# Windowed attention: x transposed by DMA on its way in, queries reordered by their evacuation

## The chip, the cores and the metric

The kernel runs on one core of a Trainium2 chip. The metric is the device time of one execution in microseconds. TensorE (PE) multiplies matrices into PSUM, VectorE (DVE), ScalarE (ACT) and GpSimd (POOL) work element by element, and SyncE (SP) issues the DMAs.

## The reference

The input x is an image of 224 x 224 positions with 96 channels in bf16. The first 48 channels of q, k and v attend within 28 horizontal windows of 8 rows each; the other 48 attend within 28 vertical windows of 8 columns each. A window has 1792 tokens.

```python
qkv = jnp.einsum('bhwc,cd->bhwd', x, wqkv)
q, k, v = qkv[..., :C], qkv[..., C:2*C], qkv[..., 2*C:]
scale = C2 ** (-0.5)                                   # C2 = C // 2 = 48, sw = 8
qh = q[..., :C2].reshape(B * nh, sw * W, C2)           # kh, vh alike: horizontal windows
ah = softmax(einsum('bqc,bkc->bqk', qh, kh) * scale)
oh = einsum('bqk,bkc->bqc', ah, vh).reshape(B, H, W, C2)
qv = q[..., C2:].reshape(B, H, nw, sw, C2).transpose(0, 2, 1, 3, 4).reshape(B * nw, H * sw, C2)
av = softmax(einsum('bqc,bkc->bqk', qv, kv) * scale)   # kv, vv alike: vertical windows
ov = einsum('bqk,bkc->bqc', av, vv)                    # put back to B, H, W, C2
o = concat(oh, ov)                                     # written there as two pads and a sum
return jnp.einsum('bhwc,cd->bhwd', o, wo)
```

## The kernel before, in words

Two windows are worked on together, one in the upper and one in the lower half of the partitions. This makes 28 pairs P: 14 horizontal ones, then 14 vertical ones. `b = P % 2` chooses between two sets of buffers.

**Preparation of a pair (`prep`).** x of the pair is loaded into `x_sb` with its tokens on the partitions (`load`, L409 to L426): two DMAs a window for a horizontal pair, 14 for a vertical one. TensorE transposes it in four fills (`pe_fn`, L534 to L540), and VectorE copies each from PSUM to `xT_sb`, where channels are on the partitions (L526 for horizontal pairs, L532 for vertical ones). The horizontal copy also reorders the tokens, from row by row to blocks of 8 x 8 positions. Because a transpose works on 64 channels at a time, with the 96 channels read as 0 to 63 and 32 to 95, `xT_sb` has 128 channel rows, and the projection weights `w_sb` have zeros and gaps to match. From `xT_sb` come keys in four fills and queries in four fills (L551; chunks of 512, 512, 512 and 256 tokens), and values in four fills (L597). VectorE evacuates them: keys with a running sum (L565), queries by a plain copy (L561), values (L602). POOL subtracts the keys' mean (L576) and scales values for the second way of taking exponentials (L610). This is 16 fills in all.

**Attention.** A score unit is one 128-key tile against 512 queries (or two tiles against 256), for both windows. TensorE computes it into one of three ring slots of PSUM, two banks each (L762). Of each pair's 49 units, 42 go to ACT, which takes the exponential (L780), and 7 to VectorE, which builds an approximate exponential out of one scaling (L804) and four cheap additions to 16-bit integers that are read as bf16 (L814). TensorE then multiplies the results by the values (L745).

**Finishing.** VectorE evacuates the output of a chunk (L709). TensorE projects it with `wo` (L637 horizontal, L666 vertical), and VectorE divides by the sums (L625, L644, L673). Horizontal results stay in `Ph_sb`; for vertical pairs POOL adds them (L677), and SP stores the rows (L686).

**What sets the order.** Every instruction is an `Op` with estimated costs. The `Planner` places the ops one after the other on each engine, by readiness and priority, and so writes out a fixed order for every engine; at run time an engine works through its list and waits for semaphores. Preparation of pair P + 1 is spread over the attention of pair P: each fill has a soft dependence on the start of one of ACT's exponentials (`pace`, L845). Fills take either an output bank or half a ring slot (`FillPool`). Loads and stores share SP's queue. `load(P + 2)` is issued when pair P's transposes have read `x_sb` (`t_pe`, L423).

Of the kernel before, what the change touches and what calls it, by code (L numbers as in the profile page):

```python
# [245 lines left out]
def bass_standalone__window_attn_cswin__vision_kernel(  # L246
# [19 lines left out]
    TH, FTH = 112, 8  # L266
    RPF = FTH * TH // W
# [6 lines left out]
    with es:  # L274
# [5 lines left out]
        ident = sb("ident", [128, 128], BF16)  # L280
        ident_f = sb("ident_f", [128, 128], FP32)
# [3 lines left out]
        x_sb = [sb(f"x_sb{i}", [128, 2, 16, C], BF16) for i in range(2)]  # L285
# [29 lines left out]
        s_x = [[[sem(f"s_x{b}{w}{hf}") for hf in range(2)] for w in range(2)] for b in range(2)]  # L315
# [70 lines left out]
        for v in range(2):  # L386
            for w in range(2):
                o_wov0 = first("dve", 0.15, lambda e, v=v, w=w: e.memset(wo_sb[v][w][:], 0.0))
        o_one = first("dve", 0.1, lambda e: e.memset(one_sb[:], 1.0))
        o_iota = first("pool", 0.3, lambda e: e.iota(ident_f[:], [[1, 128]], base=0, channel_multiplier=-1,  # L390
                                                     allow_small_or_imprecise_dtypes=True))
        o_ident = first("dve", 0.2, lambda e: e.tensor_single_scalar(ident[:], ident_f[:], 0.0, ALU.is_equal), [o_iota])
# [8 lines left out]
        x_flat = x[0].rearrange("h w c -> (h w) c")  # L401
        x_vtiles = x[0].rearrange("(kt hh) (j dw) c -> j kt hh dw c", hh=16, dw=8)
# [4 lines left out]
        t_pe = {P: [] for P in range(NP)}  # L407

        def load(P, stream):  # L409
            b = P % 2  # L410
            for w in range(2):
                src = x_flat[(2 * P + w) * NTOK:(2 * P + w + 1) * NTOK, :].rearrange("(k p) c -> p k c", p=TH) if is_h[P] else None
                for hf in range(2):
                    sm = s_x[b][w][hf]
                    own = x_tot.get((b, w, hf), 0)
                    if is_h[P]:
                        todo = [(x_sb[b][0:TH, w, hf * FTH:(hf + 1) * FTH, :], src[:, hf * FTH:(hf + 1) * FTH, :])]
                    else:
                        todo = [(x_sb[b][:, w, kt, :], x_vtiles[2 * (P - NPH) + w, kt])
                                for kt in range(8 * hf, min(NKT, 8 * hf + 8))]  # L420
                    for i, (dst, s_) in enumerate(todo):
                        op = Op("sp", 0.06, 2.2, lambda e, dst=dst, s_=s_: e.dma_start(dst, s_),
                                t_pe[P - 2] if P >= 2 and i == 0 else [], dma=(sm, own if i == 0 else 0))  # L423
                        stream.append(op)
                        x_op[(P, w, hf)] = op
                        x_tot[(b, w, hf)] = x_tot.get((b, w, hf), 0) + 16  # L426

        load(0, q_first["sp"])
        op_w0 = Op("sp", 0.7, 2.8, lambda e: e.dma_start(w_sb[0:64, :, 0:C2], wqkv.rearrange("c (s d) -> c s d", s=6)[0:64]), [o_w0], dma=(s_w0, 0))
        q_first["sp"].insert(1, op_w0)  # L430
        op_w0 = Op("sp", 0.7, 2.8, lambda e: e.dma_start(w_sb[96:128, :, 0:C2], wqkv.rearrange("c (s d) -> c s d", s=6)[64:96]), [o_w0], dma=(s_w0, 0))
        q_first["sp"].insert(2, op_w0)
# [71 lines left out]
        def prep(P, pace=None, startup=False):  # L504
# [7 lines left out]
            xt_w = {}  # L512
            qk_war = last_qk[prev2] if prev2 >= 0 else []
            pv_war = last_pv[prev2] if prev2 >= 0 else []
            xt_war = xt_read.get(prev2, [])
            xt_read[P] = []
            for w in range(2):
                for hf in range(2):
                    if is_h[P]:
                        tp, nt = TH, FTH  # L520
                        ks = [hf * FTH + j for j in range(FTH)]

                        def ev_fn(e, bk, op, w=w, hf=hf):
                            src = bk.bitcast(BF16)[:, 0:FTH * TH].rearrange("c (r bc dw) -> c r bc dw", r=RPF, dw=8)
                            dst = xT_sb[b][:, w, :].rearrange("c (bc r dw) -> c r bc dw", r=SW, dw=8)[:, hf * RPF:(hf + 1) * RPF, :, :]
                            return e.tensor_copy(dst, src)  # L526
                    else:
                        ks = list(range(8 * hf, min(NKT, 8 * hf + 8)))
                        tp, nt = 128, len(ks)

                        def ev_fn(e, bk, op, w=w, ks=ks):
                            return e.tensor_copy(xT_sb[b][:, w, ks[0] * 128:(ks[-1] + 1) * 128], bk.bitcast(BF16)[:, 0:len(ks) * 128])  # L532

                    def pe_fn(e, bk, w=w, ks=ks, tp=tp):  # L534
                        bkb = bk.bitcast(BF16)
                        for j, k in enumerate(ks):
                            for h in range(2):
                                ins = e.transpose(bkb[64 * h:64 * h + 64, j * tp:(j + 1) * tp], x_sb[b][0:tp, w, k, 32 * h:32 * h + 64],  # L538
                                                  ident[0:tp, 0:tp])
                        return ins  # L540
                    p, ops = fill(0.055 * nt, pe_fn, [x_op[(P, w, hf)], o_ident],
                                  [("dve", 0.07 + nt * tp / 1920, ev_fn, xt_war, True, dve_ev, [], None)], soft() + xt_war)
                    t_pe[P].append(p)
                    xt_w.setdefault(w, []).append(ops[0])
            xt_all = xt_w[0] + xt_w[1]
            prevk = []
            for kind in "kq":
                for c, (q0, qs) in enumerate(CH):
                    def pe_fn(e, bk, kind=kind, q0=q0, qs=qs):
                        for w in range(2):  # L550
                            ins = e.matmul(bk[64 * w:64 * w + 64, 0:qs], lhsT=w_sb[:, wblk(P, kind), :],  # L551
                                           rhs=xT_sb[b][:, w, q0:q0 + qs], start=True, stop=True)
                        return ins
                    if kind == "q":
                        if startup:
                            def ev_fn(e, bk, op, q0=q0, qs=qs):
                                return e.activation(QT_sb[b][:, q0:q0 + qs], bk[:, 0:qs], ACTF.Copy)
                            evs = [("act", 0.55, ev_fn, qk_war, True, q_first["act"], [], None)]
                        else:
                            def ev_fn(e, bk, op, q0=q0, qs=qs):  # L560
                                return e.tensor_copy(QT_sb[b][:, q0:q0 + qs], bk[:, 0:qs])  # L561
                            evs = [("dve", 0.07 + qs / 960, ev_fn, qk_war, True, dve_ev, [], None)]
                    else:
                        def ev_fn(e, bk, op, c=c, q0=q0, qs=qs):
                            return e.tensor_scalar(KT_sb[b][:, q0:q0 + qs], bk[:, 0:qs], 1.0, None,  # L565
                                                   ALU.mult, ALU.add, accum_out=ksum[b][:, c:c + 1])
                        evs = [("dve", 0.08 + qs / 960, ev_fn, qk_war, True, dve_ev, [], None)]
                        if c == NCH - 1:
                            def ev2(e, bk, op):
                                return e.tensor_scalar(kjunk[:, :], ksum[b][:, :], -1.0 / NTOK, None,  # L570
                                                       ALU.mult, ALU.add, accum_out=negmean[b][:, :])

                            def ev3(e, bk, op):
                                if startup:
                                    return e.tensor_scalar(KT_sb[b][:, :], KT_sb[b][:, :], negmean[b][:, 0:1], None, ALU.add)
                                return e.tensor_scalar(KT_sb[b][:, :], KT_sb[b][:, :], negmean[b][:, 0:1], 1.0, ALU.add, ALU.mult)  # L576
                            evs.append(("dve", 0.15, ev2, list(prevk), False, dve_ev, [], None))
                            evs.append(("dve", 0.6, ev3, [], False, dve_ev, [], None) if startup else
                                       ("pool", 1.8, ev3, [], False, pool_k, [], None))
                    p, ops = fill(0.43 * qs / 1024, pe_fn, xt_all + [op_w0], evs, soft() + qk_war)  # L580
                    xt_read[P].append(p)
                    if kind == "q":
                        q_ready[(P, c)] = ops[0]
                    else:
# [4 lines left out]
            for w in range(2):  # L589
                for k0 in range(0, NKT, VS):  # L590
                    n = min(VS, NKT - k0)

                    def pe_fn(e, bk, w=w, k0=k0, n=n):
                        for j in range(n):
                            for h in range(2):
                                t0 = (k0 + j) * 128 + 64 * h
                                ins = e.matmul(bk[64 * h:64 * h + 64, j * C2:(j + 1) * C2], lhsT=xT_sb[b][:, w, t0:t0 + 64],  # L597
                                               rhs=w_sb[:, wblk(P, "v"), 0:C2], start=True, stop=True)
# [4 lines left out]
                    p, ops = fill(0.045 * n, pe_fn, xt_w[w] + [op_w0, o_v1],  # L603
# [10 lines left out]
        xt_read = {}  # L614

# [215 lines left out]
        for P in range(NP):  # L831
# [11 lines left out]
            if P + 1 < NP:  # L843
                base = a_start[P]
                prep(P + 1, pace=lambda n, base=base: [act_of[base + int(n * NA * PACE / 16)]])  # L845
# [74 lines left out]
```

## Time and profile before

| what | value |
|---|---|
| median of 3 runs | 1147.38 us (1147.14 to 1147.86) |
| the profiled execution, its own time | 1150.81 us |
| its span in the profile | 1149.0 us |
| granted TensorE clock, mean | 0.991 |
| ACT busy | 1094.7 us |
| DVE busy | 977.8 us |
| PE busy | 1109.8 us |
| POOL busy | 198.3 us |
| DMA queue of SP, share of 16 engines | 13.8% |

Busy time is the union of an engine's instructions. Matmuls are pipelined and their ends are modelled, so a busy PE is not a PE at its peak. A group line gives the source line, the engine, what is written from what, the shape, and the count; after the bar come the busy time of the group, the mean duration of one instruction in ns, and the idle time of the engine just before such instructions with what ended it. PEld is TensorE's loading of stationary operands, which overlaps the matmuls. SPq is SP's issuing of DMAs.

### The profile page before, as it was taken

What the parts mean: (1) busy time and instruction counts of PE and PEld (TensorE: products, weight loads), DVE (VectorE), ACT (ScalarE), POOL (GpSimd) and SP (SyncE); (2) the same over time, 40 slices, a digit from 0 to 9 for tenths busy, and PEclk for the clock granted to TensorE, in tenths of its full rate; (3) what the DMA queues carried; (4) which work ended last, traced back from release to release, by engine and by line L of the source; (5) the groups of instructions that cost most, each with busy time, mean ns of one, the idle gap of its engine ahead of it and who ended that gap; (6) DMA issues with size and microseconds to landing.
All of it is one profiled execution on the core that took longest, in us unless ns stands there. A gap on an engine that the chain in (4) does not pass through costs nothing.

```text
span 1149.0 us, 30551 instructions
## 1 busy us (share of the span) xinstructions
PE 1109.8 (97%) x12888; PEld 459.3 (40%) x12888; DVE 977.8 (85%) x2138; ACT 1094.7 (95%) x1182; POOL 198.3 (17%) x256
## 2 busy tenths in 40 slices
PE   8999999999999999999999999999999999999996
PEld 3434433443443344344434433433443443344342
DVE  6898888798888978888888888898889988988974
ACT  5999999999999999999999999999999999999997
POOL 0101010010101001010112222222222313222121
PEclk7999999999999999999999999999999999999998
DMA  4011011101100110110111221121122212210011
GB/s 87 15 25 26 4 23 25 26 2 25 26 18 10 26 26 2 25 22 12 19 30 29 38 35 32 36 38 35 32 37 37 36 32 38 36 31 19 19 20 24
DMA packets 164977, 31.00 MB, mean 27 GB/s; under 512 B 164840, under 2 KB 164840, under 8 KB 164840
## 3 DMA queue, kind: packets, MB, share of 16 engines
q1 hardware_dynamic: 164840, 29.05, 13.8%
q8 instruction: 101, 1.65, 0.6%
q14 instruction: 36, 0.29, 0.1%
HBM read 19.36 MB, written 9.63 MB: 25 GB/s over the span
## 4 chain that ended last, share of the span: by engine, by line
PE 53%; DVE 25%; ACT 19%; issue 2%; DMA 0%; SPq 0%; ACTq 0%; POOL 0%; POOLq 0%
PE ps L745 24%; PE ps L762 19%; ACT PT L780 19%; DVE L_sb L814 10%; DVE Y_sb L804 7%; PE ps L538 4%; PE ps L551 3%; DVE OT_sb L709 2%; DVE KT_sb L565 2%; DVE tmp L673 2%; PE ps L597 2%; PE ps L637 1%; DVE QT_sb L561 1%; DVE V_sb L602 1%; PE ps L666 1%
## 5 line engine op out<-in xcount | busy, mean ns | idle before, releaser
L780 ACT ACTIVATE PT<-ps 128x1024 bf16<-128x1024 f32 x1176 | 1091.2, 1085 | 36.1 <-PE ps L762 26.1
L762 PE MATMUL ps<-QT_sb,KT_sb 48*128 48x512 bf16 (+1 forms) x3136 | 458.2, 357 | 8.5 <-DVE V_sb L602 1.7
L745 PE MATMUL ps<-PT,V_sb 128*64 128x512 bf16 (+1 forms) x2688 | 388.3, 360 | 0.7 <-ACT PT L780 0.7
L814 DVE TENSOR_SCALAR L_sb<-Y_sb 128x1024 int16<-128x1024 f16 x784 | 351.1, 486 | 0.7
L804 DVE TENSOR_SCALAR Y_sb<-ps 128x1024 f16<-128x1024 f32 x196 | 239.2, 1221 | 60.2 <-PE ps L762 58.2
L745 PE MATMUL ps<-L_sb,VD_sb 128*64 128x512 bf16 (+1 forms) x1792 | 270.8, 363 | 18.0 <-DVE L_sb L814 15.1
L762 PEld LDWEIGHTS ps<-QT_sb,KT_sb 48*128 48x128 bf16 x3136 | 122.0, 93 | 292.9 <-ACT PT L780 175.5
L745 PEld LDWEIGHTS ps<-PT,V_sb 128*64 128x64 bf16 x2688 | 126.9, 109 | 127.0 <-issue 104.0
L677 POOL TENSOR_TENSOR out_sb<-tmp,Ph_sb 128x384 bf16<-128x384 f32 (+1 forms) x112 | 95.5, 863 | 341.8 <-DVE tmp L673 286.5
L745 PEld LDWEIGHTS ps<-L_sb,VD_sb 128*64 128x64 bf16 x1792 | 85.5, 108 | 135.8 <-DVE L_sb L814 75.5
L576 POOL TENSOR_SCALAR KT_sb<-KT_sb,negmean 128x1792 bf16<-128x1792 bf16 x27 | 51.2, 1895 | 342.0 <-DVE rc L625 114.2
L610 POOL TENSOR_SCALAR VD_sb<-V_sb 128x256 bf16<-128x256 bf16 x112 | 51.4, 459 | 261.3 <-DVE V_sb L602 254.6
L709 DVE CAST OT_sb<-ps 128x512 bf16<-128x512 f32 x112 | 69.0, 616 | 28.7 <-PE ps L745 28.5
L551 PE MATMUL ps<-xT_sb,w_sb 128*64 128x512 bf16 x448 | 81.3, 374 | 1.1 <-DVE xT_sb L526 0.7
L565 DVE TENSOR_SCALAR_CACHE_REDUCE KT_sb<-ps 128x512 bf16<-128x512 f32 x112 | 67.7, 617 | 8.1 <-PE ps L551 7.7
L561 DVE CAST QT_sb<-ps 128x512 bf16<-128x512 f32 x108 | 66.4, 614 | 4.6 <-PE ps L551 4.6
L538 PE MATMUL ps<-ident,x_sb 112*64 112x112 bf16 (+1 forms) x1680 | 63.3, 219 | 2.4 <-DMA x_sb<-in_x_dram 1.1
L602 DVE CAST V_sb<-ps 128x480 bf16<-128x480 f32 x112 | 55.4, 500 | 10.7 <-PE ps L597 10.0
L538 PEld LDWEIGHTS ps<-ident,x_sb 112*64 112x64 bf16 (+1 forms) x1680 | 50.8, 111 | 28.1 <-issue 24.8
L673 DVE TENSOR_TENSOR tmp<-ps,rc 128x384 f32<-128x384 f32 (+1 forms) x112 | 56.3, 502 | 2.1 <-DVE rc L625 0.2
L625 DVE RECIPROCAL rc<-ps 128x4 f32<-128x4 f32 (+1 forms) x210 | 36.2, 172 | 23.2 <-PE ps L666 11.8
L644 DVE TENSOR_TENSOR Ph_sb<-ps,rc 128x384 bf16<-128x384 f32 x98 | 54.2, 553 | 1.9
(31 smaller groups left out, 315.0 us busy)
## 6 DMA issues: line engine op xcount, KB each, us to landing
x_sb<-in_x_dram SPq DMA_DIRECT2D x56, 168.0 KB, 3.5
x_sb<-in_x_dram SPq DMA_DIRECT2D x392, 24.0 KB, 2.2
out_dram<-out_sb SPq DMA_DIRECT2D x392, 24.0 KB, 1.9
wo_sb<-in_wo_dram SPq DMA_DIRECT2D x4, 9.0 KB
wo_sb<-one_sb SPq DMA_DIRECT2D x4, 0.0 KB
w_sb<-in_wqkv_dram SPq DMA_DIRECT2D x1, 36.0 KB, 2.5
w_sb<-in_wqkv_dram SPq DMA_DIRECT2D x1, 18.0 KB, 2.3
```

Source lines behind the costliest of these rows:

```text
L538: ins = e.transpose(bkb[64 * h:64 * h + 64, j * tp:(j + 1) * tp], x_sb[b][0:tp, w, k, 32 * h:32 * h + 64], ident[0:tp, 0:tp])
L551: ins = e.matmul(bk[64 * w:64 * w + 64, 0:qs], lhsT=w_sb[:, wblk(P, kind), :], rhs=xT_sb[b][:, w, q0:q0 + qs], start=True, stop=True)
L561: return e.tensor_copy(QT_sb[b][:, q0:q0 + qs], bk[:, 0:qs])
L565: return e.tensor_scalar(KT_sb[b][:, q0:q0 + qs], bk[:, 0:qs], 1.0, None, ALU.mult, ALU.add, accum_out=ksum[b][:, c:c + 1])
L673: return e.tensor_tensor(tmp[op.tok["t"]][:, 0:n, :], bk[:, 0:n * (C + 1)].rearrange("p (s c) -> p s c", s=n)[:, :, 0:C], r[:, 0:n].unsque ...
L677: return e.tensor_tensor(out_sb[b][:, w, g[0]:g[0] + n, :], tmp[hold[1].tok["t"]][:, 0:n, :], Ph_sb[:, g[0]:g[0] + n, j, :], ALU.add)
L709: return e.tensor_copy(OT_sb[b][:, q0:q0 + qs], bk[:, 0:qs])
L745: ins = e.matmul(bank(k.bank)[64 * w:64 * w + 64, 0:qs], lhsT=lhs(w, kt), rhs=rhs(w, i, qs), start=(op.tok["first"] and i == 0), stop=(k.l ...
L762: ins = e.matmul(bank(2 * s + w)[:, i * qs:(i + 1) * qs], lhsT=KT_sb[b][64 * w:64 * w + C2, kt * 128:(kt + 1) * 128], rhs=QT_sb[b][64 * w: ...
L780: a.fn = lambda e: e.activation(PT[a.tok["p"]][:].rearrange("p (s n) -> p s n", s=2), two(q.tok["s"]), ACTF.Exp, scale=scale)
L804: d.fn = lambda e: e.tensor_scalar(Y_sb[d.tok["y"]][:, :].rearrange("p (s n) -> p s n", s=2), two(q.tok["s"]), A128, Y_MIN, ALU.mult, ALU.max)
L814: t.fn = lambda e, j=j: e.tensor_scalar(L_sb[hold["l"].tok["l"]][:, j, :], Y_sb[d.tok["y"]][:, :], 127.0 * 128.0 + 128.0 * SPL_S[j], None, ...
```

## The change

The load writes `xT_sb` itself: `dma_start_transpose` takes rows of 128 values (96 of a token and 32 of what follows it) and puts value c of row t into partition c, column t. A horizontal window is one such DMA of 1792 rows, a vertical one eight DMAs of 224 rows, one for each column of the window. The last 16 rows of the image, whose 128 values would run past the end of x, are loaded by a plain DMA of 96 values with a rearranged pattern. `x_sb`, the identity matrix, the four transposing fills of a pair and their copies are gone. Tokens now lie in `xT_sb` row by row (horizontal) or column by column (vertical), and keys and values use that order. Queries still need the old order: their fills become four of 448 tokens, and the copy from PSUM to `QT_sb` writes them in place with a stride (for pair 0, the matmul reads `xT_sb` in that order instead). `load(P + 2)` waits for all twelve fills that read `xT_sb`, and the projection weights come in one DMA, ahead of x.

```diff
-        x_sb = [sb(f"x_sb{i}", [128, 2, 16, C], BF16) for i in range(2)]
...
+        def rows(first, step, n, cols):
+            return bass.AP(x.tensor, x.offset + first * C, [[step * C, n], [1, cols]])
 
         def load(P, stream):
             b = P % 2
             for w in range(2):
...
+                own = x_tot.get((b, w), 0)
+                j = 2 * P + w if is_h[P] else 2 * (P - NPH) + w
+                runs = [(j * NTOK, 1, NTOK, 0)] if is_h[P] else [(j * SW + dw, W, H, dw * H) for dw in range(SW)]
+                todo = []
+                for t0, step, n, at in runs:
+                    if t0 + (n - 1) * step == H * W - 1:
+                        n -= 16
+                        todo.append((False, xT_sb[b][0:C, w, at + n:at + n + 16],
+                                     rows(t0 + n * step, step, 16, C).rearrange("t c -> c t")))
+                    todo.append((True, xT_sb[b][:, w:w + 1, at:at + n], rows(t0, step, n, 128)))
+                for i, (tr, dst, s_) in enumerate(todo):
+                    fn = (lambda e, dst=dst, s_=s_: e.dma_start_transpose(dst, s_)) if tr else \
+                         (lambda e, dst=dst, s_=s_: e.dma_start(dst, s_, allow_slow_non_contiguous=True))
+                    op = Op("sp", 0.06, 4.0, fn, xt_read.get(P - 2, []) if i == 0 else [], dma=(s_x[b][w], own if i == 0 else 0))
...
-        q_first["sp"].insert(1, op_w0)
...
+        op_w0 = Op("sp", 0.7, 2.8, lambda e: e.dma_start(w_sb[0:C, :, 0:C2], wqkv.rearrange("c (s d) -> c s d", s=6)), [o_w0], dma=(s_w0, 0))
+        q_first["sp"].insert(0, op_w0)
...
-                    p, ops = fill(0.055 * nt, pe_fn, [x_op[(P, w, hf)], o_ident],
-                                  [("dve", 0.07 + nt * tp / 1920, ev_fn, xt_war, True, dve_ev, [], None)], soft() + xt_war)
...
-            xt_all = xt_w[0] + xt_w[1]
+            xt_all = [x_op[(P, 0)], x_op[(P, 1)]]
...
+                    moved = kind == "q" and not startup
+                    if moved:
+                        q0, qs = c * QC, QC
...
+                            if kind == "q" and startup:
+                                rhs = xT_sb[b][0:C, w, :].rearrange("c (r bc dw) -> c bc r dw", r=SW, dw=8)[:, q0 // 64:(q0 + qs) // 64]
...
-                                return e.tensor_copy(QT_sb[b][:, q0:q0 + qs], bk[:, 0:qs])
+                                if is_h[P]:
+                                    r = QC // W
+                                    dst = QT_sb[b][:, :].rearrange("p (bc r dw) -> p r bc dw", r=SW, dw=8)[:, r * c:r * c + r]
+                                    src = bk[:, 0:QC].rearrange("p (r bc dw) -> p r bc dw", r=r, dw=8)
+                                else:
+                                    d = QC // H
+                                    dst = QT_sb[b][:, :].rearrange("p (h dw) -> p dw h", dw=SW)[:, d * c:d * c + d]
+                                    src = bk[:, 0:QC].rearrange("p (dw h) -> p dw h", dw=d)
+                                return e.tensor_copy(dst, src)
...
-                prep(P + 1, pace=lambda n, base=base: [act_of[base + int(n * NA * PACE / 16)]])
+                prep(P + 1, pace=lambda n, base=base: [act_of[base + int(n * NA * PACE / 12)]])
```

## The prediction

> **What bounds the kernel now.** I read the page's engine shares first, then the groups by shape, then the table by stage (stretches of one window pair, 40.3 us), the start of the timeline, and last the DMA queues with their waits. The engine shares:
>
> ```profile
> PE 1109.8 (97%) x12888; PEld 459.3 (40%) x12888; DVE 977.8 (85%) x2138; ACT 1094.7 (95%) x1182; POOL 198.3 (17%) x256
> ```
>
> PE's 97% is not the bound by itself: a row of matmuls stays "busy" through its pipelined end. ACT's 95% is real work, and its 1176 exponentials are untouched. The groups that the change touches, and the exponentials:
>
> ```profile
> L780 ACT ACTIVATE PT<-ps 128x1024 bf16<-128x1024 f32 x1176 | 1091.2, 1085 | 36.1 <-PE ps L762 26.1 <-PE ps L745 8.8
> L561 DVE CAST QT_sb<-ps 128x512 bf16<-128x512 f32 x81 | 55.2, 681 | 4.6 <-PE ps L551 4.6
> L526 DVE COPY xT_sb<-ps 128x896 bf16<-128x896 bf16 x56 | 34.1, 619 | 15.3 <-PE ps L538 15.2
> L538 PE MATMUL ps<-ident,x_sb 112*64 112x112 bf16 x896 | 32.1, 218 | 1.3 <-DMA x_sb<-in_x_dram 1.1
> L532 DVE COPY xT_sb<-ps 128x1024 bf16<-128x1024 bf16 x28 | 19.1, 681 | 0.0
> L532 DVE COPY xT_sb<-ps 128x768 bf16<-128x768 bf16 x28 | 15.5, 553 | 8.7 <-PE ps L538 8.7
> L561 DVE CAST QT_sb<-ps 128x256 bf16<-128x256 f32 x27 | 11.2, 415 | 0.0
> ```
>
> The last two columns of L780 say the most: before its exponentials ACT sits idle 36.1 us in all, 26.1 of them because scores (L762) come late from PE. That is all that anything in the middle of the run can give back. By stage (engines' busy time and, behind it, count; then granted clock, DMA share, GB/s):
>
> ```profile
> 0.00:14.90 14.90, 11.43 (x148) 5.88 (x148) 8.85 (x31) 3.45 (x6) 0.44 (x5) 0.78 0.61 111
> 457.70:497.90 40.20, 39.53 (x468) 16.00 (x468) 35.32 (x79) 39.32 (x44) 3.85 (x5) 1.00 0.11 19
> 900.40:940.70 40.30, 38.82 (x448) 16.20 (x448) 35.01 (x77) 38.67 (x43) 10.72 (x13) 1.00 0.21 37
> ```
>
> The fourth busy time is ACT's: 39.32 of 40.20 in a horizontal stretch, 38.67 of 40.30 in a vertical one. Summed over the fourteen stretches of each half, ACT is idle 13.6 us in the horizontal half and 22.1 in the vertical one: 35.7 us. The rest of the span is 14.9 us of start and some 8 us of tail. The timeline of the start and one transposing fill at full clock (start, duration, engine):
>
> ```profile
> 0.73 0.39 SPq L422 DMA_DIRECT2D x_sb<-in_x_dram  x1
> 1.40 0.67 SPq L429 DMA_DIRECT2D w_sb<-in_wqkv_dram  x1
> 9.19 2.56 PE L551 MATMUL ps<-xT_sb,w_sb 128*64 128x512 bf16 x12 [0.72 <-DVE xT_sb L526]
> 14.93 1.02 ACT L780 ACTIVATE PT<-ps 128x1024 bf16<-128x1024 f32 x1 [1.36 <-PE ps L762]
> 15.24 0.75 PEld L538 LDWEIGHTS ps<-ident,x_sb 112*64 112x64 bf16 x16 [0.83 <-issue]
> 25.46 0.44 PEld L538 LDWEIGHTS ps<-ident,x_sb 112*64 112x64 bf16 x16 [0.42 <-issue]
> ```
>
> So x is transposed and copied by 9.13 us, keys start at 9.19, the first exponential comes at 14.93, and the first fill for pair 1 stands in PE's order at 15.24. The queues:
>
> ```profile
> q1 hardware_dynamic: 164840, 29.05, 13.8%
> x_sb<-in_x_dram SPq DMA_DIRECT2D x56, 168.0 KB, 3.5
> SPq L422 <- PE ps L745: 407.7, 21, 39.1
> ```
>
> One packet takes 13.8% x 16 engines x 1149 us / 164840 = 15.4 ns. The last line shows SP waiting at the head of a load for 407.7 us in all: loads have time to spare.
>
> **Removed.** PE: 1680 transposes in 112 fills. At full clock 16 take 0.44 us (the row at 25.46), 27.5 ns each, so 46 us. DVE: 34.1 + 19.1 + 15.5 = 68.7 us of copies, 2.4 to 2.5 us a pair. Each removed fill also gives up a PSUM half that it took from the score ring or the output banks. SP: 448 x loads become 254 (29 horizontal, 225 vertical), two weight loads become one.
>
> What of the 46 us is on the path? Only what makes ACT late. By PE's work, the fills are: transposes 46, keys and queries 224 pairs x 0.22 = 49, values and output projections 1568 matmuls each at about 30 ns (16 weight loads of the projection ran in 0.48 us) = 47 each; transposes are 46 of 189, 24%. By count they are 4 of 23.5 fills a pair, 17%. So 6 to 8.6 us of the 35.7 are theirs; I take the upper figure, because scores wait for PE's work rather than for a number of fills. DVE, which frees score slots too, loses 68.7 of 977.8, 7%: 7% of the other 27 us is 1.9. Middle: -10.5 us. Its bounds are -36 (all idle time goes) and somewhat above nothing, since the planner orders every instruction anew and may order some worse.
>
> **Moved: queries.** The count stays 108; 512 and 256 wide become 448. From 681 and 415 ns the cast costs 1.04 ns an element and 149 ns fixed, so 448 take 615 ns; 108 of them are 66.4 us, as now. Written in runs of 8 (horizontal) they should cost no more: L526 writes such runs and takes 619 ns for 896 elements, just what the slope of the dense L532 rows (553 to 681 ns for 768 to 1024, 0.5 ns each) gives, 617. Vertical writes step 16 bytes for every 2-byte element, which no row shows: between 0 extra and a doubled element time, 4 x 0.47 = 1.9 us a pair, 26 us over 14. I take 0, as the nearest row does; with the doubling DVE still gains 0.6 us a pair, so the price would be the vertical half's gain, about 5 us. The Trainium skill ("SBUF — State Buffer", the note on cachelines under Door 1: The DMA port swizzle) says that two hits per 16-byte line are needed for full bandwidth and each new line costs something; the L526 row is on the free side of that rule, and the vertical writes would be on the paying side, by an amount that the page does not give. All query chunks now become ready together, at the fourth evacuation; values are filled after that, so the next pair's start still waits for values and nothing new is last.
>
> **Added: the transposing load.** A window is 1792 rows of 256 bytes; no row shows such a DMA. Below: if rows pass like the packets now, 1792 x 15.4 ns / 16 = 1.7 us. Above: the diff cuts off the tail in blocks of 16 rows; were every block written as 32-byte pieces at a packet's price, 14336 x 15.4 / 16 = 13.8 us. Element by element it would be 221 us, and the kernel some 12 ms; only the two 16-row tails are written so. I take 3.5 us, twice the row figure (in once, out once), near the lower end since rows are what is read. The Trainium skill ("VectorE: DVE Perf Modes", The three transpose paths and Rules for kernel authors) puts one 128x128 transpose at 1309 ns on this path against 390 on TensorE, and says to use TensorE where a PSUM destination will do; that speaks against this change, and 14 such blocks in a row, an estimate, would be 18.3 us a window and the whole 1199 us. Another page of the Trainium skill ("DMA: Bandwidth & Descriptors", Latency and other measured facts) gives 261 GB/s for the same operation, an estimate of 1.76 us a window and a whole of some 1135 us.
>
> In the middle of the run T us a window is hidden: a pair's load starts when pair P's last value fill has read the buffer, near the end of attention P-1, and is needed at the first key fill for P+2, at the start of attention P+1: a full 40 us stretch for 2T = 7 us. The new wait is on 12 fills instead of 4 transposing ones, so it stands longer at the head of SP's queue; output stores queue behind it, but their buffer is reused only two pairs later. Cover gone at 2T = 40 us.
>
> At the start nothing hides it. The weight load now goes first and waits for its memset (1.40 as now), so x is issued at 2.1; with 2.0 us, the shortest time to landing seen, both windows are in at 4.1 + 2T. Against 9.13: 2T - 5. Pair 1 is in at 4.1 + 4T, and its first fill stands 6.1 us behind xT's readiness in PE's order (15.24 - 9.13): PE, which cannot pass it, waits 2T - 6.1 if positive. With T = 3.5: 2.0 + 0.9 = +2.9, say +3. At the lower end, T = 1.7, the sum is -1.6; at the upper, 22.6 + 21.5 = +44.
>
> Sum: -10.5 + 3 = -7.5. The profiled run, 1150.81 (span 1149.0), would be 1143.3; it lies 3.4 above the median of the runs, 1147.38, so I forecast 1139.9.
>
> **Rivals.** *The transfer is slow at the start* (slower): one mechanism, T, decides. The start's loss equals the middle's gain at 4T - 11.1 = 10.5, T = 5.4 us. At 13.8 us the sum is +44 - 10.5 = +33.6, 1181. For it: no row bounds T better than 1.7 to 13.8. Against: 61% DMA share in the first 14.9 us carried 1.65 MB at 111 GB/s, so the path itself is not slow. *ACT's late scores are not the transposes'* : L762 and L745 alternate whatever is filled in, the new order loses as much as it wins, and the vertical casts may double; then -3 to 0 in the middle, +3 at the start: 1147 to 1150. *Relief spreads*: a ring slot and 46 us of PE given back shorten most waits, idle falls from 36 to 10: -26 + 3, 1124. For it: L538 also stood in front of scores that were then late for several exponentials; against: vertical stretches idle most, where projections and stores are the added work, not transposes.
>
> **How the numbers follow.** Forecast 0.48 (own range 1130 to 1146), slow transfer 0.27, no gain 0.15, spread relief 0.10. A measurement of this kernel tells about 0.2% (2.3 us) from no change. Nearly all of the forecast and the relief are faster, 0.57; the no-gain case splits, so same is 0.07; slower 0.36. Range 1124 to 1181: relief at one end, the 13.8 us transfer at the other, 0.15 left out, mostly above.
>
> **What would show it.** Right: no L538 and no xT copy; ACT's idle near 25 us instead of 36.1; first exponential at 17 to 18 us; a window's load landing in 5 to 6 us; L561 at 615 ns in both halves. Wrong: keys starting after 20 us, PE waiting for x at pair 1 or later, vertical casts near 1.1 us, ACT's idle unchanged, or SP's stores late enough that POOL waits for them.

## The result, and the profile after

The changed kernel takes 1232.92 us (1229.02 to 1241.05, 4 runs) against 1147.62 us: a ratio of 1.0751, 95% interval 1.0697 to 1.0806. It is 85 us slower; 7.5 us faster was forecast, in a range up to 1181. The profiled execution took 1229.02 us, the shortest of the four; the two profiles compared below lie 78 us apart.

The engine shares and the costliest groups that answer to those shown before, from the page of the changed kernel:

```profile
PE 1118.8 (91%) x11208; PEld 437.0 (36%) x11208; DVE 1014.9 (83%) x2025; ACT 1097.3 (89%) x1182; POOL 198.2 (16%) x255
...
L761 ACT ACTIVATE PT<-ps 128x1024 bf16<-128x1024 f32 x1176 | 1093.8, 1079 | 111.9 <-PE ps L743 109.3
...
L541 DVE CAST QT_sb<-ps 128x448 bf16<-128x448 f32 x108 | 151.7, 1404 | 9.3 <-PE ps L524 9.3
```

L538 and the copies into `xT_sb` are gone, yet VectorE is busy 37 us longer, and ACT idles 111.9 us before its exponentials instead of 36.1. The query cast has become 151.7 us instead of 66.4. Its mean of 1404 ns hides two kinds; the same line, asked for in the stretch up to 560 us and in the one from 600 us on (count, then shortest, median and longest in ns):

```profile
L541 DVE CAST QT_sb<-ps x56: 609/614/2145, 29.5 to 552.7; 128x448 bf16<-128x448 f32 x56
```

```profile
L541 DVE CAST QT_sb<-ps x49: 2121/2134/2172, 598.4 to 1158.9; 128x448 bf16<-128x448 f32 x49
```

Horizontal casts take 614 ns, vertical ones 2134; the first four vertical ones fall into the first stretch, which explains its 2145. The table by stage (PE, PEld, DVE, ACT, POOL busy; clock, DMA share, GB/s) splits in the same place:

```profile
459.30:499.70 40.40, 39.26 (x412) 15.84 (x408) 33.60 (x74) 39.90 (x45) 3.99 (x6) 1.00 0.10 20
...
903.70:944.10 40.40, 34.69 (x356) 13.20 (x356) 35.21 (x64) 34.17 (x37) 9.70 (x12) 0.96 0.18 34
...
984.50:1024.90 40.40, 35.37 (x294) 12.78 (x294) 34.67 (x62) 32.26 (x35) 8.92 (x11) 0.87 0.20 38
```

The horizontal stretch is now better than before (ACT 39.90 of 40.40), the vertical ones far worse (34.17 and 32.26). From the times at which every 42nd exponential starts in the trace: horizontal pairs 1 to 12 take 470.6 us against 475.6, pairs 13 to 26 take 652.8 against 569.5. So -5 and +83 us; the first and the last pair change by +0.3 and -0.2. The loss begins with pair 13, whose attention hosts the first vertical casts. VectorE is not full there: 35.21 of 40.40.

The granted clock in the same rows, 0.96 and 0.87, is a second part of the loss. In pairs 13 to 26 the trace has fifteen stretches, 72 us in all, in which TensorE is granted half its clock; the kernel before has none there. Pair 13 has none either and still takes 44.6 us against 39.4. A straight line through the fourteen pairs gives 45.1 us and 0.30 us more for each us at half clock, so by estimate some 22 of the 83 us go with the clock and the rest with waits at full clock. What lowers the clock is not shown. But in the order written for short casts it comes and goes with the slow casts: the experiments below that are rid of them have none of it in these pairs, and the kernel before with the slow cast has 78 us.

What the casts do is seen in the timeline at 640 us, at full clock, with the rows between left out:

```profile
641.22 0.54 DVE L654 TENSOR_TENSOR tmp<-ps,rc 128x384 f32<-128x384 f32 x1
...
641.68 2.15 DVE L541 CAST QT_sb<-ps 128x448 bf16<-128x448 f32 x1
...
643.58 1.30 DVE L785 TENSOR_SCALAR Y_sb<-ps 128x1024 f16<-128x1024 f32 x1
...
644.81 2.13 DVE L541 CAST QT_sb<-ps 128x448 bf16<-128x448 f32 x1
...
646.57 1.60 DVE L795 TENSOR_SCALAR L_sb<-Y_sb 128x1024 int16<-128x1024 f16 x4
647.24 0.11 PEld L726 LDWEIGHTS ps<-L_sb,VD_sb 128*64 128x64 bf16 x2 [1.66 <-DVE L_sb L795]
...
648.67 1.02 ACT L761 ACTIVATE PT<-ps 128x1024 bf16<-128x1024 f32 x1 [1.00 <-PE ps L743]
```

The L_sb additions stand behind a 2.13 us cast in VectorE's list. TensorE's list has the product with L_sb next and waits 1.66 us for it, with scores for ACT queued behind; ACT then waits 1.00 us. The lists are fixed, so nobody may go ahead.

The load itself is quick. From the DMA issues (count, median us from issue to landing) and, behind it, from the start of the timeline:

```profile
xT_sb<-in_x_dram SPq DMA_TRANSPOSE x252, 2.5
```

```profile
2.19 8.01 SPq L417 DMA_TRANSPOSE xT_sb<-in_x_dram  x4
...
9.01 2.56 PE L524 MATMUL ps<-xT_sb,w_sb 96*64 96x512 bf16 x12 [4.35 <-issue]
...
14.74 1.02 ACT L761 ACTIVATE PT<-ps 128x1024 bf16<-128x1024 f32 x1 [1.36 <-PE ps L743]
```

The median of 2.5 us is that of the 224 vertical DMAs of up to 224 rows. The 28 horizontal ones, a window each, land 3.9 to 6.1 us after issue, median 4.7. The first four windows are issued within 8.01 us and land at 7.09, 8.92, 11.25 and 12.94 us, 1.7 to 2.3 us apart. Keys start at 9.01 us, when the second window is in, and the first exponential comes at 14.74 instead of 14.93.

### The profile page after: what moved, and what is told of

It is laid out like the page before. It is cut to its first block, busy times and chain, and to the rows that moved or that the text cites. A ratio compares the mean times of both kernels' runs of the same rounds, so it can differ in the third digit from the quotient of the medians.

```text
span 1227.2 us, 26816 instructions
## 1 busy us (share of the span) xinstructions
PE 1118.8 (91%) x11208; PEld 437.0 (36%) x11208; DVE 1014.9 (83%) x2025; ACT 1097.3 (89%) x1182; POOL 198.2 (16%) x255
## 4 chain that ended last, share of the span: by engine, by line
PE 41%; DVE 34%; ACT 21%; issue 2%; DMA 0%; ACTq 0%; POOL 0%; POOLq 0%; SPq 0%
ACT PT L761 21%; PE ps L726 21%; PE ps L743 15%; DVE Y_sb L785 10%; DVE L_sb L795 8%; DVE QT_sb L541 8%; PE ps L524 3%; DVE tmp L654 2%; DVE rc L606 1%; PE ps L647 1%; DVE Ph_sb L625 1%; DVE V_sb L585 1%; PE ps L580 1%; DVE OT_sb L690 1%; DVE KT_sb L545 1%
## 5 line engine op out<-in xcount | busy, mean ns | idle before, releaser
L761 ACT ACTIVATE PT<-ps 128x1024 bf16<-128x1024 f32 x1176 | 1093.8, 1079 | 111.9 <-PE ps L743 109.3
L743 PE MATMUL ps<-QT_sb,KT_sb 48*128 48x512 bf16 (+1 forms) x3136 | 470.1, 365 | 40.7 <-DVE QT_sb L541 20.0
L726 PE MATMUL ps<-PT,V_sb 128*64 128x512 bf16 (+1 forms) x2688 | 441.0, 369 | 0.7 <-ACT PT L761 0.7
L795 DVE TENSOR_SCALAR L_sb<-Y_sb 128x1024 int16<-128x1024 f16 x784 | 358.7, 504 | 2.1
L726 PE MATMUL ps<-L_sb,VD_sb 128*64 128x512 bf16 (+1 forms) x1792 | 289.8, 374 | 38.7 <-DVE L_sb L795 35.0
L743 PEld LDWEIGHTS ps<-QT_sb,KT_sb 48*128 48x128 bf16 x3136 | 125.3, 93 | 319.1 <-ACT PT L761 134.0
L726 PEld LDWEIGHTS ps<-PT,V_sb 128*64 128x64 bf16 x2688 | 140.5, 109 | 168.0 <-issue 144.9
L541 DVE CAST QT_sb<-ps 128x448 bf16<-128x448 f32 x108 | 151.7, 1404 | 9.3 <-PE ps L524 9.3
L524 PE MATMUL ps<-xT_sb,w_sb 96*64 96x512 bf16 (+1 forms) x448 | 84.6, 379 | 19.0 <-DVE rc L606 12.4
L580 PEld LDWEIGHTS ps<-w_sb,xT_sb 96*64 96x64 bf16 x1568 | 40.9, 116 | 23.8 <-issue 7.7
L580 PE MATMUL ps<-w_sb,xT_sb 96*64 96x48 bf16 x1568 | 44.6, 193 | 0.7
```

Of the source, the lines that this page charges most:

```text
L524: ins = e.matmul(bk[64 * w:64 * w + 64, 0:qs], lhsT=w_sb[0:C, wblk(P, kind), :], rhs=rhs, start=True, stop=True)
L726: ins = e.matmul(bank(k.bank)[64 * w:64 * w + 64, 0:qs], lhsT=lhs(w, kt), rhs=rhs(w, i, qs), start=(op.tok["first"] and i == 0), stop=(k.l ...
L743: ins = e.matmul(bank(2 * s + w)[:, i * qs:(i + 1) * qs], lhsT=KT_sb[b][64 * w:64 * w + C2, kt * 128:(kt + 1) * 128], rhs=QT_sb[b][64 * w: ...
L761: a.fn = lambda e: e.activation(PT[a.tok["p"]][:].rearrange("p (s n) -> p s n", s=2), two(q.tok["s"]), ACTF.Exp, scale=scale)
L795: t.fn = lambda e, j=j: e.tensor_scalar(L_sb[hold["l"].tok["l"]][:, j, :], Y_sb[d.tok["y"]][:, :], 127.0 * 128.0 + 128.0 * SPL_S[j], None, ...
```

## The experiments

Theory A: the stepped vertical cast is the whole loss. Rival B: the vertical loads, or query chunks that become ready together. All kernels were timed beside the kernel before on the same chip.

**Dense casts.**

```diff
-    dst = QT_sb[b][:, :].rearrange("p (h dw) -> p dw h", dw=SW)[:, d * c:d * c + d]
-    src = bk[:, 0:QC].rearrange("p (dw h) -> p dw h", dw=d)
+    dst = QT_sb[b][:, c * QC:c * QC + QC]
+    src = bk[:, 0:QC]
```

> The changed kernel, with the vertical queries' cast written densely: 448 elements in a row, so the vertical queries stand in the wrong order and that part of the computation is left out. Nothing else differs, the planner's estimates included. Theory A (the stride of the vertical cast is the whole loss): the cast takes 615 ns in both halves, ACT's idle time before its exponentials falls from 111.9 us to 15 to 30, and the time is 1147.6 less what the horizontal half gained (0.38 us a pair, 14 pairs) and about as much again in the vertical half: 1133 to 1140 us. Rival B (the loss is in the vertical loads, sixteen transposing DMAs a pair of which each holds SP for about 1.2 us ahead of the stores, or in all query chunks becoming ready together): the casts are short but the time stays above 1180 us.

Measured: 1147.49 us, ratio 0.9992 (0.9983 to 1.0001). The group of the exponentials:

```profile
L761 ACT ACTIVATE PT<-ps 128x1024 bf16<-128x1024 f32 x1176 | 1088.4, 1082 | 35.6 <-PE ps L743 32.7
```

B falls: loads and readiness are as in the changed kernel, and all 85 us are gone. A is right on the cause, wrong on the rest: it expected 1133 to 1140. ACT's idle time is 35.6 us, the old 36.1. Without the slow cast, the change is worth nothing. Horizontal pairs take 39.2 us (before: 39.6), pairs 15 to 26 take 40.9 (before: 40.8), the first one 43.2 (before: 41.5).

**Gather on the reading side.** The vertical query fill takes 56 rows of all 8 columns; the cast steps through PSUM and writes densely, in the right order.

```diff
+    elif kind == "q" and not is_h[P]:
+        hb = QC // SW
+        rhs = xT_sb[b][0:C, w, :].rearrange("c (dw h) -> c dw h", dw=SW)[:, :, q0 // SW:q0 // SW + hb]
...
+    dst = QT_sb[b][:, c * QC:c * QC + QC].rearrange("p (h dw) -> p h dw", dw=SW)
+    src = bk[:, 0:QC].rearrange("p (dw h) -> p h dw", dw=SW)
```

> The changed kernel, with the vertical queries filled as 56 rows by 8 columns a chunk, so that the cast reads PSUM with a step of 56 elements and writes QT_sb densely, in the right order. Theory A with the price on the writing side (a 2-byte write every 16 bytes): the cast takes about 615 ns and the time is that of the dense variant, 1133 to 1140 us. Rival C (any stepped access of VectorE pays, on the reading side too): the cast takes over 1.2 us and the time is over 1170 us.

Measured: 1147.02 us, ratio 0.9994 (0.9985 to 1.0002). The query casts:

```profile
L544 DVE CAST QT_sb<-ps 128x448 bf16<-128x448 f32 x108 | 66.2, 613 | 0.0
```

A step on the reading side costs nothing here (C falls); the price is on the writing side.

**The planner told.**

```diff
-    evs = [("dve", 0.07 + qs / 960, ev_fn, qk_war, True, dve_ev, [], None)]
+    evs = [("dve", 0.07 + qs / 960 if is_h[P] else 2.13, ev_fn, qk_war, True, dve_ev, [], None)]
```

> The changed kernel, with the planner told that a vertical query cast takes 2.13 us instead of 0.54; the program computes the same with the casts as slow as before, in another order. Theory D (the loss is a stale order: an order made for short casts puts matmuls that wait behind them): at least half of the 85 us comes back, under 1190 us. Rival E (the casts' own 85 us of VectorE work, 56 x 1.52, stand in front of whatever order; a cast of 2.13 us between score evacuations is longer than the three ring slots bridge): less than a quarter comes back, over 1210 us.

Measured: 1148.36 us, ratio 0.9999 (0.9990 to 1.0008). The query casts:

```profile
L541 DVE CAST QT_sb<-ps 128x448 bf16<-128x448 f32 x108 | 152.7, 1414 | 1.4 <-PE ps L524 0.6
```

They are as slow as ever, yet the whole loss is gone: D holds, beyond what it expected, and E falls. The half-clock stretches of pairs 13 to 26 shrink to one of 6.8 us. VectorE's 85 us of extra work fit into its idle time; what cost 85 us was an order written for casts of 0.54 us.

**The kernel before, with the stepped cast alone.**

```diff
...
+    if not is_h[P]:
+        dst = QT_sb[b][:, :].rearrange("p (h dw) -> p dw h", dw=SW)[:, 2 * c:2 * c + 2]
+        return e.tensor_copy(dst, bk[:, 0:448].rearrange("p (dw h) -> p dw h", dw=2))
```

> The kernel before, with TensorE's transposes and plain loads kept, and only the vertical queries' fills made 448 wide and their cast written with a step of 8 elements; the vertical queries come out in a wrong order, which leaves that part of the computation out. Theory A: casts of 2.13 us, 56 x 1.52 = 85 us more VectorE work, and since TensorE's transposes and the copies are there as well, at least as great a loss as the change's vertical half: 1225 to 1250 us. Rival B (vertical loads): under 1180 us.

Measured: 1221.78 us, ratio 1.0645 (1.0620 to 1.0669). This is A's answer and not B's, a little under its range: without any transposing load the stepped cast costs 74 us. (The vertical query fills are 448 wide here too, and their chunks become ready together; the dense variant has both and loses nothing.)

**The kernel before, once more.** No edit.

> The kernel before, unchanged, profiled again. Its first profiled execution took 1150.81 us, 3.4 above the median of its runs. If this profile comes out near 1147, the stage times of before get a second reading: theory F (the 0.38 us a horizontal pair that the changed kernel seemed to gain is a real gain) expects 42 horizontal exponentials every 39.5 to 39.6 us here as well; rival G (the first profile was a slow one) expects 39.2 to 39.4.

Measured: 1148.78 us. Its horizontal pairs 1 to 12 take 475.6 us again, so F holds: the horizontal gain is real, 0.4 us a pair. But its first pair takes 39.5 us instead of 41.5, and that is the whole difference between the two profiles of before. In the gather variant it takes 42.4. The matmul rows show the difference (TensorE in the gather variant, then in the second profile of before; four score matmuls, 512 wide):

```profile
17.68 1.04 PE L746 MATMUL ps<-QT_sb,KT_sb 48*128 48x512 bf16 x4
```

```profile
17.50 0.60 PE L762 MATMUL ps<-QT_sb,KT_sb 48*128 48x512 bf16 x4 [0.30 <-ACT PT L780]
```

At the start TensorE runs either at full pace or, until some 20 to 24 us, at about half. This is where the two profiles of before part: between 15 and 20 us the granted clock is 0.50 in the first and 1.00 in the second. All nine kernels with transposing loads run at half pace there, after TensorE stood idle for 4.2 to 4.9 us before the keys, and have first pairs of 41.7 to 43.2 us. Of the five profiles without such loads, where TensorE is idle for 0.7 us there, three run at full pace (first pairs of 39.5 us) and two at half (41.5 and 42.4). So the half pace goes with the pause but comes without it too, and its cause stays open.

**Gather in TensorE's read.** The moving operand steps 448 bytes; the vertical fills are 512 and 256 wide again, and the cast is the old dense one.

```diff
+    rhs = xT_sb[b][0:C, w, :].rearrange("c (dw h) -> c h dw", dw=SW)[:, q0 // SW:(q0 + qs) // SW]
```

> The changed kernel, with the vertical queries put in order by TensorE's reading instead of the cast: the moving operand is read with 8 columns 448 bytes apart, one 2-byte value from each, and the cast is dense as in the kernel before. If a step costs TensorE nothing, the matmuls stay at 376 ns, the order holds and the time is that of the PSUM gather, 1145 to 1149 us. If TensorE pays for it as VectorE does (4.4 times an element's time), 56 pairs of matmuls take some 0.9 us each instead of 0.22, 38 us more PE work in an order that does not know of it: over 1170 us.

Measured: 1152.88 us, ratio 1.0040 (1.0026 to 1.0053), between the two expectations. The projection matmuls of keys and queries from 640 to 1100 us, shortest, median and longest:

```profile
L526 PE MATMUL ps<-xT_sb,w_sb x176: 296/498/1040, 652.2 to 1084.9; 96*64 96x512 bf16 x132, 96*64 96x256 bf16 x44
```

The longest takes 1040 ns against 404 in the kernel before: TensorE pays for such a step too, but only 4.4 us of time follow.

**Pairs of elements.**

```diff
+    dst = QT_sb[b][:, :].rearrange("p (h dw) -> p h dw", dw=SW)[:, :, d * c:d * c + d]
+    src = bk[:, 0:QC].rearrange("p (dw h) -> p h dw", dw=d)
```

> The changed kernel with its order and with the same 448 vertical queries a cast, but the cast goes row by row and writes the two columns of a row one after the other: 224 pieces of 4 bytes every 16 bytes, where the changed kernel writes 448 of 2 bytes; PSUM is read with a step of 224 elements. Theory J (the price is for each 16-byte piece of QT_sb newly touched: 2134 - 615 = 1519 ns / 448 = 3.4 ns): 615 + 224 x 3.4 = 1375 ns a cast. Rival K (the price is for each element of a stepped write): 2134 ns as before and the time of the changed kernel. With J the time lies between: the order stays that of short casts; if the loss goes with the cast's excess, half of 85 us, 1185 to 1195 us; if three ring slots bridge a shorter cast, less.

Measured: 1147.07 us, ratio 0.9991 (0.9982 to 1.0001). The vertical casts:

```profile
L541 DVE CAST QT_sb<-ps x48: 605/611/617, 620.0 to 1079.5; 128x448 bf16<-128x448 f32 x48
```

Both theories missed. Two neighbours written one after the other, every 16 bytes, cost nothing extra; J's price for a newly touched piece is not the rule as stated.

**Steps of 1 to 32 elements.**

```diff
+    S = (1, 2, 4, 8, 16, 32, 8)[(P - NPH) // 2]
...
+    dst = QT_sb[b][:, :].rearrange("p (h s) -> p s h", s=S)
...
```

Each cast writes 448 elements of this view.

> The changed kernel, with the vertical queries' cast written at steps of 1, 2, 4, 8, 16 and 32 elements (2 to 64 bytes) in turn, two pairs each; the queries stand in wrong orders, which leaves that part of the computation out. Only the casts' durations are looked at. Theory J (the price is for each 16-byte piece newly touched): steps 1, 2 and 4 touch 1/8, 1/4 and 1/2 as many pieces as elements, so 615 to 1.4 us, step 8 takes 2.13 us and steps 16 and 32 no more than that. Rival K (any step costs the full price): 2.13 us from step 2 on. Rival L (the price goes on with the distance): over 2.5 us at steps 16 and 32.

Its one run took 1199.48 us. The casts by step, each on a line of its own (L549 step 1, L551 step 2, L553 step 4, L555 step 8, L557 step 16, L558 step 32; shortest, median, longest):

```profile
L555 DVE CAST QT_sb<-ps x16: 2124/2141/2170, 786.0 to 1129.3; 128x448 bf16<-128x448 f32 x16
L549 DVE CAST QT_sb<-ps x8: 610/614/615, 539.8 to 588.4; 128x448 bf16<-128x448 f32 x8
L551 DVE CAST QT_sb<-ps x8: 645/650/653, 619.5 to 669.7; 128x448 bf16<-128x448 f32 x8
L553 DVE CAST QT_sb<-ps x8: 1134/1146/1152, 701.4 to 753.8; 128x448 bf16<-128x448 f32 x8
L557 DVE CAST QT_sb<-ps x8: 2024/2044/2078, 883.5 to 942.6; 128x448 bf16<-128x448 f32 x8
L558 DVE CAST QT_sb<-ps x8: 2089/2112/2128, 975.6 to 1034.6; 128x448 bf16<-128x448 f32 x8
```

K and L fall. For single stepped elements, 149 ns + 4.45 ns for each 16-byte piece gives 647, 1146 and 2143 ns at steps 2, 4 and 8, as measured, and nothing is added beyond. Only the pairs, 224 pieces at no extra price, don't fit; why is open. The Trainium skill ("SBUF — State Buffer", the note on cachelines) says that full bandwidth needs at least two hits on each 16-byte line, and that each new line costs something. The pairs, with two hits a line, are free; but step 4, with two hits a line as well, takes 1146 ns, so two hits are not enough here. The pairs of windows that host these casts take 39.2 us (step 1), 41.0 (step 2), 42.3 (step 4) and 45.6 to 50.8 from step 8 on, against 40.9 with dense vertical casts: in this order a cast of nearly twice the time costs 1.4 us a pair, one of 3.5 times 4.7 to 9.9. TensorE has stretches at half clock only in the latter pairs, 3.4 to 17.1 us in each.

**Where the expected gain went.** In the dense variant TensorE no longer runs the 1680 transposes, which the prediction put at 46 us, VectorE is busy 43 us less (977.8 to 935.0), and ACT idled as before. A row of the trace that the prediction did not use is L_sb's, for the kernel before and the gather variant:

```profile
L814 DVE TENSOR_SCALAR L_sb<-Y_sb x784: 386/418/1621, 18.4 to 1135.4; 128x1024 int16<-128x1024 f16 x196
```

```profile
L798 DVE TENSOR_SCALAR L_sb<-Y_sb x784: 388/421/1910, 18.4 to 1131.3; 128x1024 int16<-128x1024 f16 x196
```

The same addition takes 418 ns or four times that. In the trace of the dense variant the 544 that overlap no POOL instruction take 419 ns on average and 428 at most. The 51 that overlap POOL's KT_sb subtraction take 901 on average, beside its out_sb additions it is 706, beside its VD_sb products 554. Each of the 27 subtractions catches one addition that then ends 0.28 us after it. The Trainium skill ("SBUF — State Buffer", SBUF: two separate sides) says that a VectorE operation in a two-port mode and a GpSimd operation exclude each other for a whole instruction; these ends agree. Theory H: these collisions, of which the planner does not know, swallow the gain.

```diff
-    evs.append(("dve", 0.6, ev3, [], False, dve_ev, [], None) if startup else
-               ("pool", 1.8, ev3, [], False, pool_k, [], None))
+    evs.append(("dve", 0.6, ev3, [], False, dve_ev, [], None))
```

> The PSUM gather variant, with the subtraction of the keys' mean (L556 on POOL, 27 x 1.9 us) done by VectorE, as pair 0 does it (0.69 us each). Theory H (the PE and DVE time that the change gives back is lost again to VectorE's additions into L_sb, which take 420 ns alone and up to 1910 ns beside POOL's KT_sb subtraction, in an order that does not know of it): the longest L_sb addition falls to about 1.2 us, ACT's idle time falls by the 1.1 us a vertical pair that follows the subtraction, about 15 us, less something for 27 x 0.69 = 19 us more VectorE work; 1130 to 1140 us. Rival I (ACT's idle time in the vertical half has another cause): 1145 us or more.

> The kernel before, with the same subtraction moved from POOL to VectorE. Theory H: the collisions cost the kernel before less (its L_sb additions beside KT_sb lost 21 us in all, against 25 in the dense variant) and its VectorE has 69 us more to do, so it gains less than the PSUM gather variant does, 0 to 8 us: 1139 to 1148 us; the difference to that variant is then what the transposing load is worth when nothing else swallows it. Rival I: no difference between the two variants' gains.

Measured: the gather variant 1118.97 us, ratio 0.9739 (0.9726 to 0.9752); the kernel before 1132.47 us, ratio 0.9862 (0.9848 to 0.9875). Both beat every expectation. The exponentials and L_sb of the gather variant:

```profile
L761 ACT ACTIVATE PT<-ps 128x1024 bf16<-128x1024 f32 x1176 | 1084.5, 1154 | 10.1 <-PE ps L743 9.5
```

```profile
L795 DVE TENSOR_SCALAR L_sb<-Y_sb x784: 388/420/1143, 18.5 to 1102.6; 128x1024 int16<-128x1024 f16 x196
```

ACT idles 10.1 us, and with these orders the transposing load is worth 13.5 us. But the planner also wrote a new order. The last two kernels keep the order and only shorten POOL's instruction:

```diff
-    return e.tensor_scalar(KT_sb[b][:, :], KT_sb[b][:, :], negmean[b][:, 0:1], 1.0, ALU.add, ALU.mult)
+    return e.tensor_scalar(KT_sb[b][:, 0:64], KT_sb[b][:, 0:64], negmean[b][:, 0:1], 1.0, ALU.add, ALU.mult)
```

> The PSUM gather variant with its order on every engine unchanged and the subtraction of the keys' mean still on POOL, but over 64 of the 1792 keys, so that POOL is done in a fraction of the 1.9 us; the subtraction of the mean from the other keys is left out. Moving the subtraction to VectorE brought 28 us, but it also made the planner write a new order. Theory H (it was the collision of VectorE's L_sb additions with POOL's subtraction): most of those 28 us come back in the old order as well, 1115 to 1127 us. Rival M (it was the new order): 1140 us or more.

> The kernel before with the same shortening (the mean is taken off 64 of the 1792 keys; order unchanged). Theory H: the kernel before, too, is freed of the collisions and comes to 1128 to 1138 us, and the gap to the variant above is what the transposing load is worth without them, near the 10.5 us of the prediction's middle. Rival M: 1143 us or more.

Measured: 1132.09 us, ratio 0.9865 (0.9849 to 0.9882), and 1132.71 us, ratio 0.9868 (0.9853 to 0.9883). For the kernel before, H's figure; for the gather variant, between H and M. The L_sb additions of the gather variant, now:

```profile
L798 DVE TENSOR_SCALAR L_sb<-Y_sb x784: 390/421/1141, 18.6 to 1116.3; 128x1024 int16<-128x1024 f16 x196
```

The 36 beside the shortened subtraction take 436 ns on average, and the wait of 0.73 us that ACT had at one fixed place of each of pairs 15 to 26 is gone, 8.8 us of the 15. That keys come earlier is not the reason: in neither kernel's trace does an instruction wait for POOL's subtraction. So the collisions with the subtraction cost either kernel about 15 us. In the old order the load is worth 0.6 us even without them, which is within the spread of the runs; the other 13 us of the best variant are left to its new order, in which ACT idles 10.1 us instead of 24.2. This contradicts the idea that the collisions swallowed the load's gain: they are a loss of their own, about the same in both. What the new order does better was not separated further.

## Why the prediction was wrong, by its own steps

**The step that failed: the vertical cast's upper bound and its price.** The prediction saw that no row shows a 2-byte write every 16 bytes, bounded it by a doubled element time (615 to 1085 ns), took the lower end as nearest, and priced the upper end at 5 us in all. The cast took 2134 ns, and the price of a doubling was too low by four (casts of 1146 ns, above): 1.4 us a pair, 20 us over 14. Two errors, then. The doubling was an invented end, not one from a row; the skill's rule, cited beside it, spoke for paying with no amount, and was not allowed to widen the range. And the price was made from VectorE's sum of work ("VectorE still gains 0.6 us a pair"), where the loss came from waits in a fixed order: with the order rewritten, the same casts cost nothing. That such waits would come with TensorE at half clock was in no term.

**Nothing new is last.** Wrong for the same reason. What is late is not the next pair's start but VectorE's next additions and score evacuations, and through TensorE's list the scores for ACT. Once in every pair from 13 to 26, a third of the way in, scores also wait for a vertical cast itself, 1.7 to 1.9 us against 0.2 to 0.4 in the dense variant.

**The middle, -10.5.** In the dense variant the horizontal pairs 1 to 13 gave 5.2 us, the vertical half gave nothing, and the first pair took back 1.7 to 3.7 us, by which profile of before it is compared with. Idle time was shared out by TensorE's work. But ACT's waits stand at a few fixed places of each pair (in the gather variant with the short subtraction, before the same three exponentials of each of pairs 15 to 26), set by the order, while TensorE itself waits for ACT's ring slots, 175.5 us in the kernel before:

```profile
L762 PEld LDWEIGHTS ps<-QT_sb,KT_sb 48*128 48x128 bf16 x3136 | 122.0, 93 | 292.9 <-ACT PT L780 175.5 <-issue 57.9 <-DVE Y_sb L804 7.7
```

Taking work from an engine that waits shortened no wait there.

**The start, +3.** Measured -0.2 for the first exponential: 4.1 + 2T = 9.0 makes T 2.4 us, not 3.5. Of the two figures cited, 1.76 us is near and 18.3 far off. The prediction had no term for issuing: SP is busy 1.6 to 2.5 us with each of the first four windows, about as long as they land apart, so whether the issue or the transfer sets the pace is open. The wait for pair 1 did not appear (2T - 6.1 is negative). The prediction also had no term for the half-paced matmuls of the first pair, which every kernel with transposing loads showed, and before in the first of its two profiles.

**Right:** the load is hidden in the middle; the first two windows land 4.9 and 5.1 us after issue (5 to 6 forecast); horizontal casts at 614 ns (615 forecast); no engine waited for a load or a store there; the warning sign "vertical casts near 1.1 us" pointed at the right line. **The rivals:** slow transfer fell. *ACT's late scores are not the transposes'* came nearest: it describes the dense and gather variants, and named the vertical casts, with far too small a price.

## What to carry to other kernels

A duration that is unknown to a fixed order can cost as much as all its extra work, here 85 us for 85, where a planner that knows it hides all of it: measure the instruction first, then tell the planner, and only then judge the change. An access with a step that no row shows has no upper bound until it is measured; turn the step to the reading side, or write at least two neighbours together, where that can be had. Before counting on relief for one engine, look whether it waits itself, and whether instructions of one kind differ fourfold in duration: here that spread pointed at 15 us that the change was not about.

## What the runs showed of the hardware

- VectorE casting PSUM to bf16: 614 ns for 448 elements; 650, 1146 and 2141 at write steps of 4, 8 and 16 bytes, 2044 and 2112 at 32 and 64; runs of two (every 16 bytes) or eight neighbours, or a step of 56 elements in the PSUM read, cost nothing.
- VectorE's 16-bit addition over 1024 elements: 419 ns alone, up to 1910 beside a POOL instruction of 1.8 to 2.1 us, 0.28 us after whose end it ends.
- A transposing load of 1792 rows of 256 bytes: 3.9 to 6.1 us from issue to landing, the first four in a row 1.7 to 2.3 us apart; one of 224 rows: 2.5 us.
- TensorE reading single elements every 448 bytes: up to 1040 ns for a 512-wide projection matmul against 404.
- TensorE's granted clock: 72 us at half in the vertical half with slow casts in an order written for short ones, 6.8 with the same casts in an order that knows them, none with short casts.
